# Gates and ups of a GEGLU FFN as pairs of 64-row half tiles, beside a sliding-window attention

## The chip, the cores and the metric

The kernel runs on one core of one Trainium2 chip. The metric is the device time of one execution in microseconds. TensorE (PE) multiplies matrices, VectorE (DVE), ScalarE (ACT) and GpSimd (POOL) work element by element, and SyncE (SP) issues DMAs. Each engine works through its own instructions in order. TensorE writes to PSUM, which has eight banks of 128 partitions by 512 float32.

## The reference

The input x is 2048 rows of D = 448, in bfloat16. It is normalised once, and both halves of the sum read the normalised rows.

```python
xn  = layernorm(x)                                 # no scale, no shift
q, k, v = split(xn @ wqkv)                         # H = 16 heads, Dh = 28
scores  = einsum("bhqd,bhkd->bhqk", q, k) * Dh ** -0.5
mask    = (i - j >= 0) & (i - j < 256)             # sliding window of 256 keys
o       = softmax(where(mask, scores, -1e9)) @ v
ffn     = (gelu_tanh(xn @ w_gate) * (xn @ w_up)) @ w_down    # F = 1792
out     = x + o @ wo + ffn
```

## The kernel before, in words

The work goes in four blocks of 512 query rows (`qb`), one behind the other. Activations lie transposed: `xnT` holds xn with its features on the partitions, in four chunks. 448 features are three chunks of 128 and a rest of 64; the rest's 64 rows are stored in both halves of the fourth chunk. Each block has two parts.

*Attention* (`attention`, lines 536 to 662). A loop over steps, 10 in blocks 1 to 3 and 12 in block 0. A step's scores (L616) go to one tile of four banks, ScalarE takes their exp (L622) to `p_sb`, and masks follow on VectorE (L523) or, in block 0, on GpSimd (L533). There is one such score tile, so the scores of a step wait for the exp of the step before. At fixed steps (`pvs`) the product with v of a group of four heads is issued (`pv`, L576). From block 1 on it has two accumulators, one for each half of the keys, which ScalarE copies (L560) and VectorE adds (L561). These two are issued at once, or put in the list `behind`, which `flush` empties behind the next exp or gated multiply: group 2 in every block, and group 3 in block 3 alone. What depends on the sums (L548 to L556, and L542 on GpSimd) comes some steps later. Between the steps TensorE gets other work from feeds (`Feed`, generators that yield an estimate in ns behind each piece): in block 0 the rest of its q and k projections, some early ups and the projections of block 1; in blocks 1 and 2 the output projection and down matmuls of the block before (`gen_down`, L375 and L380) and the next block's projections; in block 3 the down of block 2 and early ups. `share` deals out the pieces by the estimates, with a share for each step (`want`) and a plan for the second feed (`plan`). What is left behind the last scores is drained at once.

*The gated part* (`gated`, L418 to L486). F = 1792 is 14 tiles of 128 columns, taken in pairs of neighbours (f, f + 1). Gates go to a tile of two banks (`gt`), ups to two single banks (`u0`). ScalarE takes the gelu of both gates (L464), and VectorE multiplies with the ups (L471), or with early ups already in `hT` (L469), where `gen_up` has had them copied by VectorE (L415). Early are f = 2, 4, 8 in block 0 and f = 2, 4, 6, 8, 10 in block 3. `last_v` issues the last PV group within the gated part, behind the first gates and ups. Behind each pair, `hook` issues what is left of the attention and, up to block 2, what the next blocks need: DMAs that gather and spread parts of k (`collect`, `deliver`), and in the first two blocks normalised rows and their DMA transposes.

A gate or up tile has a contraction of 448: three matmuls of 128 rows by 512 columns (`mm3`, L232) and one of 64 rows (`mm_half`, L238). Two such halves in the upper and lower 64 rows of the array run at the same time, and the kernel puts halves of two tiles next to each other. In blocks 1 to 3 the first pair's halves are cut to 32 columns of weights (m = 32), the shape of the PV matmuls behind them. The half's weights of w_gate and w_up lie in two tiles, `wgu3` and `wug3`.

*PSUM.* Four banks for scores and gates ("s"), two "m", one "o", one "d". `bank` takes the next name from a list (`ring`): in block 0 ("m", "m", "d"), later "m" alone. In block 0 the PV always uses "o". After block 3 comes its own down (`gen_down`), a check of the softmax sums, and an alternative path for unusual inputs, which isn't run here.

The loads of x and weights are DMAs on SP's queue, a few small ones on ScalarE's, in the order of the code. Transposes of the first four row tiles are done by TensorE (`transp`), later ones by DMA.

Of the kernel before, what the change touches and what calls it, by code (L numbers as in the profile page):

```python
# [9 lines left out]
ALU = mybir.AluOpType  # L10
# [6 lines left out]
P = 128  # L17
# [58 lines left out]
def kernel(  # L76
# [45 lines left out]
    def rows(w, c0, n):  # L122
        return w[c0 * P:(c0 + n) * P, :].rearrange("(c p) n -> p c n", p=P)

# [19 lines left out]
    nc.sync.dma_start(out=wu[:, :, :], in_=rows(B_w_up, 0, 3))  # L144
    nc.sync.dma_start(out=wug3[0:64, :], in_=B_w_up[384:448, :])
    nc.sync.dma_start(out=wgu3[64:128, :], in_=B_w_up[384:448, :])
# [34 lines left out]
    xnT = const.tile([P, 4, S], bf16, name="xnT")  # L181
    qT = const.tile([P, 4, S], bf16, name="qT")
# [174 lines left out]
    UP1 = 1660  # L357
    STEP, PV = 450, 870
# [35 lines left out]
    def half(ps, f, gate, hi, ts, start, stop, m=P):  # L394

        w3 = wgu3 if gate != bool(hi) else wug3
        mm_half(ps, w3[:, f * P:(f + 1) * P], xnT[:, 3, ts], hi, start, stop, m)

    def three(ps, f, gate, ts, start, stop):
        w = wg if gate else wu  # L400
        mm3(ps, lambda c: w[:, c, f * P:(f + 1) * P], lambda c: xnT[:, c, ts], start, stop)

    def gen_up(qb, fs):

        ts = slice(qb * QB, (qb + 1) * QB)
        for f in fs:
            us = []
            for i in range(2):
                us.append(bank("ue"))
                three(us[i][:, :], f + i, False, ts, True, False)  # L410
                yield (650, HOLD) if i else 650
            for i in range(2):
                half(us[i][:, :], f + i, False, i, ts, False, True)
            for i in range(2):
                nc.vector.tensor_copy(out=hTs[qb][:, f + i, :], in_=us[i][:, :])  # L415
            yield -360

    def gated(qb, early, last_v, flush, hook):  # L418

        ts = slice(qb * QB, (qb + 1) * QB)  # L420
        hT = hTs[qb]
        turn = ["o" if down_tag[0] == "d" else "d", down_tag[0]] * 4

        def single(name, tag):
            return psum.tile([P, QB], f32, name=name, tag=tag, bufs=2 if tag == "m" else 1)[:, :]

        def begin(f, apart=False):
            last_tag[0] = turn[0] if f not in early else last_tag[0]
            pr = dict(f=f, us=[])
            if apart:  # L430
                pr["gs"] = [single("g0", tag) for tag in ("m", turn.pop(0))]
                return pr
            pr["gt"] = phase[0].pool.tile([P, 2, QB], f32, name="gt", tag="s")
            pr["gs"] = [pr["gt"][:, i, :] for i in range(2)]
            if f not in early:
                tags = ("m", turn.pop(0))
                if qb == 0 and f == 0:
                    tags = [ring[0][(ring[1] + i) % 3] for i in range(2)]
                    if "d" in tags:
                        turn.insert(0, "o")  # L440
                pr["us"] = [single("u0", tag) for tag in tags]
            return pr

        def dense(pr, start):
            f = pr["f"]
            gs = [(g, f + i, True) for i, g in enumerate(pr["gs"])]
            us = [(u, f + i, False) for i, u in enumerate(pr["us"])]
            for ps, fi, gate in (gs + us if f else us + gs):
                three(ps, fi, gate, ts, start, not start)

        def halves(pr, start, m):
            f = pr["f"]
            for i in range(2):
                if pr["us"]:
                    half(pr["gs"][i], f + i, True, 0, ts, start, not start, m)
                    half(pr["us"][i], f + i, False, 1, ts, start, not start, m)
                else:
                    half(pr["gs"][i], f + i, True, i, ts, start, not start, m)

        def end(pr):  # L460
            f = pr["f"]
            ge = work.tile([P, 2, QB], bf16, name="ge", bufs=2)
            if "gt" in pr:
                nc.scalar.activation(out=ge[:, :, :], in_=pr["gt"][:, :, :], func=ACT.Gelu_apprx_tanh)  # L464
            else:
                for i, g in enumerate(pr["gs"]):
                    nc.scalar.activation(out=ge[:, i, :], in_=g, func=ACT.Gelu_apprx_tanh)
            if not pr["us"]:
                nc.vector.tensor_tensor(out=hT[:, f:f + 2, :], in0=ge[:, :, :], in1=hT[:, f:f + 2, :], op=ALU.mult)  # L469
            for i, u in enumerate(pr["us"]):  # L470
                nc.vector.tensor_tensor(out=hT[:, f + i, :], in0=ge[:, i, :], in1=u, op=ALU.mult)  # L471
                flush()
            hook(f)

        for fs in ((0, 2), (4, 8, 6), (10, 12)) if qb in (0, 3) else ((0,), (2, 4), (6, 8), (10, 12)):
            prs = [begin(fs[0])]
            dense(prs[0], True)
            prs += [begin(f, len(fs) == 3 and f == fs[1]) for f in fs[1:]]
            for pr in prs:
                halves(pr, pr is not prs[0], 32 if qb and not fs[0] else P)  # L480
            if not fs[0]:
                last_v()
            end(prs[0])
            for pr in prs[1:]:
                dense(pr, False)
                end(pr)  # L486
# [49 lines left out]
    def attention(qb, feeds, aux, plan):  # L536
# [30 lines left out]
        def pv(g):  # L567

            tags = ("o",) if not qb else ("m", "m" if g < 3 else down_tag[0])
# [22 lines left out]
        pvs = {4: 0, 6: 1, 9: 2} if qb else {4: 0, 7: 1, 10: 2}  # L592
        for i, (scores, ncol, edges) in enumerate(steps):
# [111 lines left out]
    transp(3, nc.vector.tensor_copy, "d")  # L705
    pvs.append(alone("pv", "o"))
# [17 lines left out]
    ring[1] = 0  # L724
# [20 lines left out]
    def loads():  # L745

        nc.sync.dma_start(out=x_sb[:, 12:16, :], in_=xv[:, 12:16, :])
        nc.sync.dma_start(out=wgu3[0:64, :], in_=B_w_gate[384:448, :])
        nc.sync.dma_start(out=wug3[64:128, :], in_=B_w_gate[384:448, :])
        nc.sync.dma_start(out=wg[:, :, :], in_=rows(B_w_gate, 0, 3))  # L750
# [7 lines left out]
    for qb in range(NB):  # L758
# [80 lines left out]
    with tc.If(n_ok < 1, preferred_fallthrough_block=True, label="general"):  # L839
        general_path(tc, locals_=dict(x_sb=x_sb, xnT=xnT, qT=qT, kT=kT, v_sb=v_sb, wg=wg, wu=wu, wgu3=wgu3, wd=wd, wo=wo,  # L840
                                      ident=ident, outv=outv))


def general_path(tc, locals_):
# [4 lines left out]
    with ExitStack() as st:  # L849
# [11 lines left out]
        for qb in range(NB):  # L861
            ts = slice(qb * QB, (qb + 1) * QB)
            for f in range(NF):
                fs = slice(f * P, (f + 1) * P)
                pg = ps.tile([P, QB], f32, name="pg", tag="pg")
                pu = ps.tile([P, QB], f32, name="pu", tag="pu")
                for i, (dst, w) in enumerate(((pg, L["wg"]), (pu, L["wu"]))):
                    for c in range(3):
                        nc.tensor.matmul(dst[:, :], lhsT=w[:, c, fs], rhs=xnT[:, c, ts], start=(c == 0), stop=False)
                    p0 = 64 * i  # L870
                    nc.tensor.matmul(dst[:, :], lhsT=L["wgu3"][p0:p0 + 64, fs], rhs=xnT[p0:p0 + 64, 3, ts], start=False, stop=True,
                                     tile_position=(p0, 0))
# [78 lines left out]
```

## Time and profile before

| | |
|---|---|
| median of 3 runs | 220.65 us (220.32 to 220.88) |
| the profiled execution | 221.15 us, of which the span is 219.4 |
| mean granted TensorE clock | 0.996 |
| TensorE busy | 213.9 us, 2287 matmuls |
| VectorE, ScalarE, GpSimd busy | 152.1, 133.3, 46.9 us |
| exp (L622) | 42 times, 73.8 us in all |
| gelu (L464) | 26 times, 1.02 us each |
| copy of a PV accumulator (L560) | 12 times, 0.58 us each |
| copy of an early up (L415) | 16 times, 10.2 us in all |
| DMA | 13.30 MB, engines busy mostly in the first 45 us |

The span is what the trace shows from the first instruction to the last; the execution's own time has 1.7 us around it. "Issue" in the lists of waits is time in which an engine waited for nothing that the profile shows. A line that names a helper (L232, L238) stands for all that call it, so groups are told apart by their tiles: `gt` gates, `u` ups, `ue` early ups, `po` output and down, `sc` scores, `ov` PV. PEld is TensorE's loading of weights, which runs beside the matmuls.

### The profile page before, as it was taken

To read this page: it belongs to the slowest core of one execution; us is meant where nothing else is said; L and a number is where in the kernel's file an instruction comes from. 1 tells how busy PE (TensorE), PEld (TensorE's weight loads), DVE (VectorE), ACT (ScalarE), POOL (GpSimd) and SP (SyncE) were. 2 spreads that over 40 slices of the span, in tenths; PEclk is the share of its full clock that TensorE was granted. 3 is DMA by queue.
4 is the path that set the end of the run, shared out by engine and by line. 5 is a ranking of instruction groups with operands and counts; after the bars stand their busy time and mean duration, and the time that the engine had idled before them with its cause. 6 is when DMAs were issued, how large, how long until landed. Compare 5 with 4: busy or idle time off the path is not lost.

```text
span 219.4 us, 5447 instructions
## 1 busy us (share of the span) xinstructions
PE 213.9 (98%) x2287; PEld 96.1 (44%) x2287; DVE 152.1 (69%) x346; ACT 133.3 (61%) x131; POOL 46.9 (21%) x80
## 2 busy tenths in 40 slices
PE   7999999999999999999999999999999999999993
PEld 2433333434444454444444445444344445444562
DVE  6787896799666883679565795386356799479521
ACT  3588788662878875432878888233486777565000
POOL 5377987320000120022000022022000022022001
PEclk9999999999999999999999999999999999999998
DMA  6993799104200001102300000200000000000011
GB/s 193 310 311 71 188 325 302 30 4 72 45 3 21 24 24 27 20 3 46 60 13 24 23 1 24 52 13 0 0 3 21 25 3 24 24 1 0 22 35 37
DMA packets 18045, 13.30 MB, mean 61 GB/s; under 512 B 8704, under 2 KB 16992, under 8 KB 18016
## 3 DMA queue, kind: packets, MB, share of 16 engines
q1 hardware_dynamic: 17072, 12.62, 21.1%
q8 instruction: 19, 0.31, 0.6%
q10 hardware_dynamic: 944, 0.29, 0.5%
q14 instruction: 10, 0.08, 0.1%
HBM read 9.15 MB, written 2.18 MB: 52 GB/s over the span
## 4 chain that ended last, share of the span: by engine, by line
PE 96%; ACT 1%; DVE 1%; issue 1%; DVEq 0%
PE po L380 20%; PE gt L232 16%; PE u L232 12%; PE sc L616 6%; PE po L375 6%; PE gt L238 5%; PE ue L232 5%; PE ov L576 5%; PE pq L232 4%; PE pv L232 4%; PE pk L232 3%; PE wps L191 2%; PE pq L238 1%; PE g L232 1%; PE ue L238 1%; PE pv L238 1%
## 5 line engine op out<-in xcount | busy, mean ns | idle before, releaser
L622 ACT ACTIVATE p_sb<-sc 128x2048 bf16<-128x2048 f32 (+2 forms) x42 | 73.8, 1758 | 12.6 <-PE sc L616 8.2
L380 PE MATMUL po<-wd,hT 128*128 128x448 bf16 (+1 forms) x238 | 49.8, 342 | 0.0
L464 ACT ACTIVATE ge<-gt 128x1024 bf16<-128x1024 f32 x26 | 26.6, 1024 | 34.9 <-PE u L238 20.1
L542 POOL TENSOR_TENSOR oN<-oc,l 128x512 bf16<-128x512 f32 x12 | 16.0, 1334 | 137.8 <-DVE l L556 87.4
L232 PE MATMUL gt<-xnT,wg 128*128 128x512 bf16 x156 | 37.5, 380 | 0.0
L471 DVE TENSOR_TENSOR hT<-ge,u 128x512 bf16<-128x512 bf16 x40 | 25.7, 682 | 12.9 <-ACT ge L464 12.9
L380 PEld LDWEIGHTS <-hT 128*128 128x128 bf16 x238 | 21.5, 98 | 18.8 <-issue 2.6
L232 PE MATMUL u<-xnT,wu 128*128 128x512 bf16 x120 | 29.2, 379 | 0.0
L523 DVE TENSOR_TENSOR p_sb<-p_sb,masks 128x256 bf16<-128x256 bf16 (+1 forms) x90 | 26.8, 353 | 0.4 <-ACT p_sb L622 0.4
L232 PEld LDWEIGHTS <-wg 128*128 128x128 bf16 x168 | 15.3, 98 | 21.3 <-issue 4.5
L232 PEld LDWEIGHTS <-wu 128*128 128x128 bf16 x168 | 16.0, 98 | 19.2 <-issue 1.0
L561 DVE TENSOR_TENSOR oc<-oc,ov 128x512 f32<-128x512 f32 x12 | 8.2, 687 | 16.5 <-ACT oc L560 16.5
L616 PE MATMUL sc<-qT,kT 28*64 28x320 bf16 (+7 forms) x640 | 16.9, 263 | 0.2
L415 DVE CAST hT<-ue 128x512 bf16<-128x512 f32 x16 | 10.2, 681 | 8.4 <-PE ue L238 8.3
L375 PE MATMUL po<-wo,oN 128*128 128x448 bf16 (+1 forms) x68 | 15.9, 343 | 0.0
L385 DVE TENSOR_TENSOR res<-po,x_sb 128x448 bf16<-128x448 f32 (+1 forms) x17 | 10.0, 586 | 8.6 <-PE po L380 8.4
L533 POOL TENSOR_SCALAR_AFFINE_SELECT p_sb<-p_sb 128x512 bf16<-128x512 bf16 (+1 forms) x20 | 14.2, 730 | 5.0 <-ACT p_sb L622 4.8
L238 PE MATMUL gt<-xnT,wgu 64*128 64x512 bf16 (+1 forms) x67 | 12.7, 380 | 0.0
L560 ACT COPY oc<-ov 128x512 f32<-128x512 f32 x12 | 7.0, 583 | 8.8 <-PE ov L576 8.8
L232 PE MATMUL pq<-xnT,wqp 128*128 128x512 bf16 x45 | 12.2, 380 | 0.1
L548 DVE STREAM_TRANSPOSE l<-oc 128x512 f32<-128x512 f32 x16 | 11.3, 704 | 1.4 <-POOL oN L542 1.2
L232 PE MATMUL ue<-xnT,wu 128*128 128x512 bf16 x48 | 12.0, 380 | 0.0
(97 smaller groups left out, 241.9 us busy)
## 6 DMA issues: line engine op xcount, KB each, us to landing
out_dram<-res SPq DMA_DIRECT2D x15, 112.0 KB
x_sb<-in_A_x_dram SPq DMA_DIRECT2D x3, 448.0 KB
wu<-in_B_w_up_dram SPq DMA_DIRECT2D x1, 1344.0 KB
wg<-in_B_w_gate_dram SPq DMA_DIRECT2D x1, 1344.0 KB
wd<-in_B_w_down_dram SPq DMA_DIRECT2D x3, 448.0 KB
wraw<-in_A_wqkv_dram SPq DMA_DIRECT2D x2, 252.0 KB
wo<-in_A_wo_dram SPq DMA_DIRECT2D x4, 98.0 KB
wv<-in_A_wqkv_dram SPq DMA_DIRECT2D x1, 336.0 KB
```

Of the source, the lines that this page charges most:

```text
L232: nc.tensor.matmul(ps, lhsT=lhs(c), rhs=rhs(c), start=start and c == 0, stop=stop and c == 2, skip_group_check=True)
L238: nc.tensor.matmul(ps[c:c + m], lhsT=lhs[p0:p0 + 64, c:c + m], rhs=rhs[p0:p0 + 64], start=start, stop=stop, tile_position=(p0, c), skip_gr ...
L375: nc.tensor.matmul(po[:, 0:w], lhsT=oN[:, g, cs], rhs=wo[:, g, lo:up], start=(g == 0), stop=False, skip_group_check=True)
L380: nc.tensor.matmul(po[:, 0:w], lhsT=hT[:, f, cs], rhs=wd[:, f, lo:up], start=False, stop=(f == NF - 1), skip_group_check=True)
L464: nc.scalar.activation(out=ge[:, :, :], in_=pr["gt"][:, :, :], func=ACT.Gelu_apprx_tanh)
L471: nc.vector.tensor_tensor(out=hT[:, f + i, :], in0=ge[:, i, :], in1=u, op=ALU.mult)
L523: nc.vector.tensor_tensor(out=reg, in0=reg, in1=m, op=ALU.mult)
L533: nc.gpsimd.affine_select(out=reg, in_=reg, pattern=mid + [[1 if diag else -1, min(w, P)]], compare_op=ALU.is_ge, fill=0.0, base=0 if diag ...
L542: nc.gpsimd.tensor_tensor(out=oN[:, g, :], in0=oc[:, :], in1=inv, op=ALU.mult)
L548: nc.vector.transpose(out=l1[:, :, :].rearrange("p a b -> p (a b)"), in_=oc[:, :])
L616: nc.tensor.matmul(ss[k0:k0 + nk, j, col:col + nq], lhsT=kT[r, g, kt * P + k0:kt * P + k0 + nk], rhs=qT[r, g, qb * QB + q0:qb * QB + q0 + ...
L622: nc.scalar.activation(out=p_sb[:, :, 0:ncol], in_=ss[:, :, 0:ncol], func=ACT.Exp, scale=SCALE)
```

## The change

Gates and ups are no longer three matmuls of 128 rows and one of 64, but seven of 64 rows. F is cut in halves: tile p (0 to 6) pairs with tile p + 7. The weights of tile p lie in partitions 0 to 63 and those of p + 7 in partitions 64 to 127, each as seven chunks of 64 features. `chunk` issues the two matmuls of one chunk, one in each half of the array.

Each of the two needs the same 64 features of x, but in its own half of the partitions. Chunk c lies in only one half of `xnT`, so the other half comes from `xsw`, a copy of the block's x with the halves of the partitions exchanged, which two DMAs from SBUF to SBUF make (`swap`): in block 0 on ScalarE's queue, right behind the fourth transpose; in blocks 1 to 3 on SP's, ahead of the block's attention. There is one `xsw`, so each swap waits for the last reader of the one before.

Further:
- `load_ffn` loads w_up and w_gate by two DMAs each instead of three.
- Early are pairs 1, 2, 4 in block 0 and 1, 2, 3 in block 3. An early up takes both its banks at the start.
- The gated part's order is new: gates first, then ups, pair by pair, with pair 0 and pair 1 next to the last PV; the 32-column halves are gone.
- Block 0's ring has four banks behind its first six places, and its PV takes its bank from there. Its feed mixes early ups and v projections in another order.
- PV groups 2 and 3 go to `behind` in every block.
- Estimates, block 3's plan and the formula of the share in block 3 have other constants; the run of the first feed at the start of the attention is gone.

```diff
-    wg = const.tile([P, 3, F], bf16, name="wg")
-    wu = const.tile([P, 3, F], bf16, name="wu")
-    wgu3 = const.tile([P, F], bf16, name="wgu3")
-    wug3 = const.tile([P, F], bf16, name="wug3")
+    wg = const.tile([P, 7, F // 2], bf16, name="wg")
+    wu = const.tile([P, 7, F // 2], bf16, name="wu")
...
+    def load_ffn(dst, w):
+        wv64 = w.rearrange("(c p) n -> p c n", p=64)
+        for hi in range(2):
+            nc.sync.dma_start(out=dst[64 * hi:64 * hi + 64, :, :], in_=wv64[:, :, hi * (F // 2):(hi + 1) * (F // 2)])
...
-    UP1 = 1660
-    STEP, PV = 450, 870
+    UP1 = 1600
+    STEP, PV = 450, 700
...
+    def swap(qb, queue):
+        ts = slice(qb * QB, (qb + 1) * QB)
+        for hi in range(2):
+            queue.dma_start(out=xsw[64 * hi:64 * hi + 64, :, :], in_=xnT[64 - 64 * hi:P - 64 * hi, 0:3, ts])
+
+    def chunk(pair, w, p, qb, c):
+        for hi, ps in enumerate(pair):
+            r = slice(64 * hi, 64 * hi + 64)
+            ts = slice(qb * QB, (qb + 1) * QB)
+            x = xnT[r, 3, ts] if c == 6 else xnT[r, c // 2, ts] if c % 2 == hi else xsw[r, c // 2, :]
+            nc.tensor.matmul(ps, lhsT=w[r, c, p * P:(p + 1) * P], rhs=x, start=c == 0, stop=c == 6,
+                             tile_position=(64 * hi, 0), skip_group_check=True)
...
+        for p in ps:
+            us = [bank("ue")[:, :] for _ in range(2)]
+            for c in range(7):
+                chunk(us, wu, p, qb, c)
...
+                nc.vector.tensor_copy(out=hTs[qb][:, p + 7 * i, :], in_=us[i])
...
+        up(0)
+        gate(0)
+        end(0)
+        gate(1)
+        if 1 in early:
+            end(1)
+            gate(2)
+            up(2)
+        else:
+            gate(2)
+            up(1)
+            end(1)
+            up(2)
+        end(2)
+        for p in range(3, 7):
+            gate(p)
+            up(p)
+            end(p)
...
-            tags = ("o",) if not qb else ("m", "m" if g < 3 else down_tag[0])
+            if not qb:
+                ring[1] += 1
+            tags = (ring[0][ring[1] - 1],) if not qb else ("m", "m" if g < 3 else down_tag[0])
...
-                if g == 2 or qb == NB - 1 and g == 3:
+                if g > 1:
                     behind.append((oc, ov))
...
-        if qb:
-            feeds[0].run()
...
-                want = (whole - late) / (left + 0.2) + late - ahead - to
+                want = (whole - late) / (left + (0.2 if qb < NB - 1 else -0.4)) + late - ahead - to
...
-                share(feeds, want, to)
+                if qb == NB - 1:
+                    share(feeds[:1], want, 0)
+                    share(feeds, 0, to)
+                else:
+                    share(feeds, want, to)
...
     transp(3, nc.vector.tensor_copy, "d")
+    swap(0, nc.scalar)
...
-    ring[1] = 0
+    ring[:] = ["m", "m", "d"] * 2 + ["m", "o", "m", "d"] * 8, 0
...
-            early = (2, 4, 8)
+            early = (1, 2, 4)
...
-                          (gen_up(0, (2, 8)), 2 * UP1), (gen_proj(1), PROJ), (gen_up(0, (4,)), UP1))]
+                          (gen_up(0, (1,)), UP1), (gen_v(1, (4,)), 1500), (gen_up(0, (4,)), UP1), (gen_v(1, (6,)), 1500),
+                          (gen_up(0, (2,)), UP1), (gen_qk(1, range(4)), PROJ - 3000))]
...
-                early = (2, 4, 6, 8, 10)
+                early = (1, 2, 3)
...
-                plan = {0: 1300, 2: 1300, 4: 1300, 6: 1300, 7: 1300}
+                plan = {1: 1280, 2: 1280, 7: 1280}
+        if qb:
+            swap(qb, nc.sync)
```

More of the change, by code (lines that the diff above doesn't have):

```diff
@@ L143 @@
     nc.gpsimd.memset(v_sb[:, :, :, Dh + 1:32], 0.0)
[L144 to L146 removed]
+    load_ffn(wu, B_w_up)
     nc.sync.dma_start(out=x_sb[:, 8:12, :], in_=xv[:, 8:12, :])
@@ L181 @@
     xnT = const.tile([P, 4, S], bf16, name="xnT")
+    xsw = const.tile([P, 3, QB], bf16, name="xsw")
     qT = const.tile([P, 4, S], bf16, name="qT")
@@ L392, in new_hT @@
         hTs[qb] = hT
[L394 to L403, printed above, removed]
-        ts = slice(qb * QB, (qb + 1) * QB)
-        for f in fs:
-            us = []
-            for i in range(2):
[L409 to L416, printed above, removed]
+    def swap(qb, queue):
+        ts = slice(qb * QB, (qb + 1) * QB)
+        for hi in range(2):
+            queue.dma_start(out=xsw[64 * hi:64 * hi + 64, :, :], in_=xnT[64 - 64 * hi:P - 64 * hi, 0:3, ts])
@@ L421, in gated @@
         hT = hTs[qb]
         turn = ["o" if down_tag[0] == "d" else "d", down_tag[0]] * 4
[L424 to L464, printed above, removed]
-            else:
[L466 to L486, printed above, removed]
+        if not qb:
+            first = [ring[0][ring[1]], ring[0][ring[1] + 1]]
+            ring[1] += 2
+            turn = ["o" if "d" in first else "d", "d" if "d" in first else "o"] * 4
@@ new lines, in gated, with up, gate @@
+        us, ges = {}, {}
+        def up(p):
+            if p in early:
+                return
+            last_tag[0] = turn[0]
+            tags = ("m", turn.pop(0)) if qb or p else first
+            us[p] = [psum.tile([P, QB], f32, name="u0", tag=tag, bufs=2 if tag == "m" else 1)[:, :] for tag in tags]
+            for c in range(7):
+                chunk(us[p], wu, p, qb, c)
+        def gate(p):
+            gt = phase[0].pool.tile([P, 2, QB], f32, name="gt", tag="s")
+            for c in range(7):
+                chunk([gt[:, i, :] for i in range(2)], wg, p, qb, c)
+            if not p:
+                last_v()
+            ges[p] = work.tile([P, 2, QB], bf16, name="ge", bufs=2)
+            nc.scalar.activation(out=ges[p][:, :, :], in_=gt[:, :, :], func=ACT.Gelu_apprx_tanh)
@@ new lines, in end @@
+        def end(p):
+            ge = ges.pop(p)
+            if p in early:
+                nc.vector.tensor_tensor(out=both(hT, p), in0=ge[:, :, :], in1=both(hT, p), op=ALU.mult)
+            else:
+                for i, u in enumerate(us.pop(p)):
+                    nc.vector.tensor_tensor(out=hT[:, p + 7 * i, :], in0=ge[:, i, :], in1=u, op=ALU.mult)
+                    flush()
+            hook(2 * p)
+        up(0)
[11 more added lines that the diff above has]
+            up(2)
```

32 lines of the change are left out of this document (20 added, 12 removed).

## The prediction

> **What bounds the kernel now.** I read the page first: the busy shares, then the chain that ended last.
>
> ```profile
> span 219.4 us, 5447 instructions
> PE 213.9 (98%) x2287; PEld 96.1 (44%) x2287; DVE 152.1 (69%) x346; ACT 133.3 (61%) x131; POOL 46.9 (21%) x80
> PE 96%; ACT 1%; DVE 1%; issue 1%; DVEq 0%
> ```
>
> TensorE is busy 98% of the span and carries 96% of the chain. So a change pays only through fewer or shorter TensorE slots, and costs whatever it makes TensorE wait. Next the waits of TensorE's weight loads:
>
> ```profile
> PEld L238 <- issue: 16.8, 41, 0.4
> PEld L616 <- issue: 8.3, 32, 0.4
> PEld L232 <- issue: 6.8, 22, 0.4
> PEld L576 <- issue: 4.2, 12, 0.4
> ```
>
> Hardly any is a wait for another engine: they are "issue", and they come where the tile shape changes: L238 is the 64-row half, L616 the scores, L576 PV. What one costs is seen in TensorE's timeline in the gated part of block 0:
>
> ```profile
> 43.76 0.81 PE L232 MATMUL gt<-xnT,wg 128*128 128x512 bf16 x3
> 44.51 0.39 PE L238 MATMUL gt<-xnT,wgu 64*128 64x512 bf16 x1
> 44.51 0.39 PE L238 MATMUL gt<-xnT,wug 64*128 64x512 bf16 x1
> 44.73 0.38 PE L238 MATMUL g<-xnT,wgu 64*128 64x512 bf16 x1
> 44.74 0.38 PE L238 MATMUL g<-xnT,wug 64*128 64x512 bf16 x1
> 44.95 0.38 PE L238 MATMUL gt<-xnT,wgu 64*128 64x512 bf16 x1
> 44.95 0.38 PE L238 MATMUL u<-xnT,wgu 64*128 64x512 bf16 x1
> 45.16 0.38 PE L238 MATMUL gt<-xnT,wgu 64*128 64x512 bf16 x1
> 45.17 0.38 PE L238 MATMUL u<-xnT,wgu 64*128 64x512 bf16 x1
> 45.48 0.39 PE L232 MATMUL g<-xnT,wg 128*128 128x512 bf16 x1
> ```
>
> Columns: start, duration, instruction. Two 64-row matmuls start together and the next pair follows about 0.216 us later: a pair costs one slot, the same as a dense 128-row matmul of 512 columns (three in 0.81 with the last one's 0.38: 0.216 apart). From dense to pair it is 0.31 (the third dense starts at 44.19, the pair at 44.51), from pair to dense again 0.31 (45.17 to 45.48): a change of shape costs some 0.1.
>
> Last, the end of block 3's attention, all engines:
>
> ```profile
> 184.04 0.43 PE L616 MATMUL sc<-qT,kT 28*64 28x320 bf16 x24
> 184.40 2.82 PE L380 MATMUL po<-wd,hT 128*128 128x448 bf16 x14
> 184.64 1.88 ACT L622 ACTIVATE p_sb<-sc 128x2048 bf16<-128x2048 f32 x1 [0.83 <-PE sc L616]
> 186.41 0.58 ACT L560 COPY oc<-ov 128x512 f32<-128x512 f32 x1
> 187.02 0.69 DVE L561 TENSOR_TENSOR oc<-oc,ov 128x512 f32<-128x512 f32 x1 [0.56 <-ACT oc L560]
> 187.06 0.38 PE L232 MATMUL u<-xnT,wu 128*128 128x512 bf16 x1
> ```
>
> After the last scores, the first up needs the bank of PV group 2, which ScalarE empties (L560) only behind its last exp: 187.06 - 184.04 = 3.02 us. Fourteen output matmuls cover it just so; nothing is idle.
>
> **The slots.** Before, a pair of F tiles takes 2 x 6 dense slots and 2 paired ones, 14 in all; after, 2 x 7 paired ones, 14 again. Slot for slot the change gains nothing: 392 slots either way over the four blocks.
>
> **The switches (a gain).** From the order of the instructions, shape changes fall from 161 to 140. Mean extra gap of each kind, from the starts in the trace: dense to 64-row 99 ns (12 fewer: 1.19 us), back 99 (9 fewer: 0.89), dense to PV 96 (3 fewer: 0.29), 64x32 to dense 147 (3 fewer: 0.44), block-0 scores to dense 113 (3 fewer: 0.34), one each of block-0 PV to dense (113) and dense to scores (96): 0.21. Removed 3.36. Added are eleven, of kinds that mostly have no row; each is priced by the sibling with dense in the place of 64-row: 3 x 113, 3 x 147, 3 x 96, 1 x 113, 1 x 106 = 1.29 (bounds: all 96, 1.06; all 147, 1.62). Net -2.07; a first slot behind a switch is also 10 ns long, 21 x 10 = 0.21. Sum -2.28, bounds -1.9 to -2.6.
>
> **Weight loads.** Each slot now has two 64-row loads of 93 ns (group L238) in place of one of 98. I take 0: the shown pairs run on at 0.216 with such loads beside them. But those chains are four slots long, and the new ones 7 to 42. Bounds: 0, and for loads wholly exposed 336 slots that were dense x 93 ns = 31 us. I stay by the chain, which is the same operation.
> The Trainium skill, "TensorE: Matmul & The Clock Gate", Part 3, "What overlaps and what doesn't", says that a weight load overlaps running matmuls only when it targets another row group; here both row groups are busy, so by that rule the 31 us would show. This trace's 0.216 between pairs speaks against it.
>
> **The start and block 0 (a loss).** The ring of four banks makes the first projection of group 1 wait for VectorE's copy of the second v tile (12.58 + 0.61, from the timeline) where it had waited for ScalarE's of the first, and the one behind it moves along: 0.1 to 0.25, part of it within two waits that are there now (0.17 at 14.97, 0.12 at 15.37): +0.15. Between scores 4 and 5 the filler is 1.85 us against 0.39 + 1.45 + 0.05 that one exp and its hand-over take: +0.05 to 0.09. An early up's second matmul follows ScalarE's v copy: +0.08. Together +0.3 (0.1 to 0.5).
>
> **Copies by DMA (nothing).** Block 0's swap is two issues on ScalarE's queue, 0.40 to 0.55 us each by its earlier issues; they fall between VectorE's copy of the last transpose (9.47 + 0.42) and the statistics that ScalarE waits for until 11.41. Behind them stands only that rstd. Its 384 packets of 1 KB at 46 to 126 ns on 16 engines are 1.1 to 3.0 us more beside the up weights, which land by 16.33; the first early up is at 19.49. Cover left: 0.16 at least. Two DMAs of wu (1.8 KB packets) move the bytes of three before; 0.9 KB and 3.6 KB packets have nearly one rate (16 to 21 bytes/ns). Transposes 6 and 7, now behind the swap's semaphores on SP, are issued at 20.41 or later: 0. Blocks 1 and 2 read their swap 30 us later. Block 3's is issued when the last up of block 2 has run; the first early up comes 4.1 us behind that by the new order. Two issues of 0.5, then an output row's 1.68 from issue to landing plus 0.2 to 1.2 for the larger size: landed 2.4 to 3.4 us behind. Cover 0.7; I take 0, bounds 0 to 0.9. SP has only output stores queued behind it, the first of them later than this.
>
> **Block 3 (the main loss).** Early ups fall from five pairs to three: 2 x 7 slots of 0.216, 3.02 us, less filler under the attention's ten exps, which stay as they are (the two pairs' ups come later, in the gated part). Three places follow:
> - The second early pair starts close behind the first and, its halves running together, needs both banks "m" at once, so both VectorE copies (two L415, 1.29 us in a row) must be over; before, the next up began with one bank, and waited 0.10 (at 179.68). +0.58 (bounds 0.1 to 0.7).
> - Step 6 to 7 has 2.36 to 2.41 us of filler against 0.73 + 1.88 + 0.06 = 2.67 of hand-over and exp: +0.25 (0.18 to 0.35, with step 7).
> - The first up still waits for L560's copy, 3.02 after the last scores, but only six output matmuls are left as cover: scores 0.36 + 6 x 0.19 + 0.1 = 1.60. +1.35 (1.28 to 1.42). The filler was spent in earlier steps, the new share divides by left - 0.4 in place of left + 0.2.
> Together +2.18.
>
> **Blocks 1, 2 and the rest (nothing).** Cover behind their last scores is 3.54 against 3.02. The copies put behind a gelu delay group 3's sum by some 1 us; ScalarE idles 34.9 us ahead of its gelus, and the output projection that reads it comes a block later (in block 3, six gelus later). Without that cover it would cost one L560 and one L561, 1.27. VectorE's mults of early pairs are still one instruction each.
>
> **Sum.** -2.28 + 0.30 + 2.18 = +0.20. The profiled run took 221.15 (span 219.4 and 1.7 around it), 0.5 above the median of 220.65. So 221.35 in such a run, 220.85 as median.
>
> **Rivals.** A measurement of this kernel tells a change from none at about 0.3%, 0.66 us: 219.99 to 221.31 is "same".
> - *A, the forecast*: gain and waits cancel; 220.85, with its bounds 219.9 to 221.8.
> - *B, block 3 doesn't wait*: if ScalarE's copy isn't what the first up needs (another bank) and the copies of the early pairs keep up and the steps aren't short, the gain is left with the start's loss: -2.28 + 0.30 = 218.7; with half the waits 219.8. For it: the present block 3 has waits of 0.1 only. Against: 3.02 us hang on one exp and one copy, and the filler is counted.
> - *C, slower through the swapped copy in block 3*: TensorE takes its work in order, so each us that it lands past 4.1 us behind its release is a us on the end. Landing at 5.5 gives 222.2, at 7 223.7. For it: 1 KB packets here take 46 to 126 ns, over twice apart, and nothing shows an on-chip copy of this size. Against: the cover of 0.7. It decides from 4.6 us on.
> - *D, long chains of pairs run slower than 0.216*: 392 slots, so 4 ns more in each is 1.6 us, 222.4; 10 ns 3.9, 224.7; it decides from 1.2 ns on. Against: the four shown. Its far end, every load exposed, is 220.85 + 31 = 252; I give that 0.02 of D's 0.17.
> That far end is what the Trainium skill's page named above would have.
>
> **Chances.** A 0.46, B 0.24, C 0.13, D 0.17. A gives 0.02 faster, 0.36 same, 0.08 slower; B 0.23 faster and 0.01 same; C 0.13 and D 0.16 slower, 0.01 same. Faster 0.25, same 0.38, slower 0.37. Forecast 220.85. A's own range is 219.9 to 221.8; to hold 8 in 10 it must take in most of B and the near half of C and D: 218.7 to 222.6.
>
> **What will show it.** Shape changes: the L238-like issue waits fall, and pairs stand 0.216 apart in chains of any length (else D). The waits page should have a wait of TensorE's first up on ScalarE's oc copy of 1.3 us in block 3, and of an early up on VectorE's hT copy of 0.6 (else B); a wait on the swapped copy's DMA would be C. ScalarE's and VectorE's busy times should stay within 1 us. I'm wrong if block 3's attention doesn't lose about 2 us to waits, or the rest doesn't gain 2.

## The result, and the profile after

The changed kernel takes 223.39 us (median of 6 executions, 222.35 to 223.75) against 220.58 for the kernel before: 1.0116 times, 95% interval 1.0092 to 1.0141. It is slower, and above the range. The profiled execution took 223.43, span 221.6; that of before had 221.15 and 219.4. So the two profiled executions differ by 2.3 us, and their spans by 2.1, where the forecast had 0.2. (The profiled execution of before happened to lie 0.5 above its median, which is why the medians stand further apart.) In some kernels below single executions have a mean granted clock of 0.99 and take 1 to 4 us more; the ratios leave out those that are over 1.5% above the fastest of their kernel.

The page of the changed kernel:

```profile
span 221.6 us, 6054 instructions
PE 212.8 (96%) x2581; PEld 98.3 (44%) x2581; DVE 150.3 (68%) x344; ACT 132.9 (60%) x129; POOL 47.1 (21%) x80
PE 86%; DVE 5%; DMA 5%; ACT 2%; issue 2%; ACTq 0%; DVEq 0%
```

TensorE is busy 1.1 us less than before, and its share fell from 98% to 96%: what it saved, it waits, and more. In the chain stands a DMA with 5%, where there was none. The waits of TensorE's matmuls (who waited, for whom: us in total, times, longest) name the places:

```profile
PE wps L196 <- DVE wo L172: 1.4, 1, 1.4
PE u L413 <- ACT oc L563: 1.3, 1, 1.3
PE ue L413 <- DMA xsw<-xnT: 0.8, 1, 0.8
PE pq L237 <- DVE v_sb L263: 0.5, 2, 0.2
PE pv L237 <- DVE hT L431: 0.2, 1, 0.2
PE sc L619 <- ACT p_sb L625: 0.2, 1, 0.2
PE ue L413 <- DVE hT L431: 0.2, 1, 0.2
```

Only the first line was there before. The third is one that the prediction did not have. It stands in block 0 (timeline; start, duration, instruction):

```profile
19.55 0.40 PE L619 MATMUL sc<-qT,kT 28*128 28x128 bf16 x8
19.88 0.39 PE L413 MATMUL ue<-xnT,wu 64*128 64x512 bf16 x1
21.06 0.39 PE L413 MATMUL ue<-xsw,wu 64*128 64x512 bf16 x2 [0.79 <-DMA xsw<-xnT]
21.28 0.39 PE L413 MATMUL ue<-xnT,wu 64*128 64x512 bf16 x2
21.49 0.39 PE L413 MATMUL ue<-xsw,wu 64*128 64x512 bf16 x2
```

The first half of the pair needs only xnT and goes at 19.88. Its partner needs the swapped copy, and comes at 21.06. The two are 1.18 us apart: 0.96 of lost time, and one slot of 0.216 that runs alone, since the halves stay one step out of line until the end of the tile. The copy had been issued at 10.0 (ScalarE's timeline, then the piece of the chain):

```profile
10.02 1.54 ACTq L403 DMA_DIRECT2D xsw<-xnT  x2
11.61 0.30 ACT L206 ACTIVATE lnv<-mv_all,eps_t 128x2 f32<-128x2 f32 x1 [2.16 <-DVE mv_all L202]
```

```profile
10.73 10.20 DMA xsw<-xnT
```

10.2 us lie between the second issue and the landing at 20.93. The forecast had put the copy beside the weights at a cost of 1.1 to 3.0 us of their engines' time. In the packets of the trace, w_up's go from 9.35 to 18.88, and the copy's first one starts at 16.57, 5 us after it was issued; the last ends at 20.37. A packet of w_up, 1.8 KB, took 144 ns in the median, as long as one of 3.6 KB before the change (140).

The landing is not the end of the packets. In the traces a DMA raises its semaphore sixteen times, and TensorE goes on after the last: here fifteen of them stand by 20.64 and the last at 20.93, 0.56 behind the last packet.

The two issues took 1.54 us, not 0.8 to 1.1. At the start stands a wait on VectorE's copy of v. The first line is the changed kernel's; the second is from a kernel below (e7) in which ScalarE issues no DMA there:

```profile
13.29 0.81 PE L237 MATMUL pq<-xnT,wqp 128*128 128x512 bf16 x3 [0.22 <-DVE v_sb L263]
12.40 0.81 PE L237 MATMUL pq<-xnT,wqp 128*128 128x512 bf16 x3
```

In the first, VectorE's copy ends at 13.24; in the second it runs until 12.69, and the projection starts ahead of its end, right behind ScalarE's copy (12.35). So the projection waits for another engine in the two programs.

Block 3's end is as forecast:

```profile
183.36 0.43 PE L619 MATMUL sc<-qT,kT 28*64 28x320 bf16 x24
183.73 1.31 PE L385 MATMUL po<-wd,hT 128*128 128x448 bf16 x6
183.96 1.88 ACT L625 ACTIVATE p_sb<-sc 128x2048 bf16<-128x2048 f32 x1 [0.95 <-DVE l L559]
185.73 0.58 ACT L563 COPY oc<-ov 128x512 f32<-128x512 f32 x1
186.36 0.37 PE L413 MATMUL u<-xnT,wu 64*128 64x512 bf16 x1 [1.33 <-ACT oc L563]
```

From the last scores to the first up it is 3.00 us again, six output matmuls cover 1.6 of it, and TensorE stands for the rest.

Summed over the starts of the matmuls, waits and lone slots are 4.8 us after and 0.6 before, and the rest of the gaps fell by 2.2. Together that is +2.0 up to the last matmul, and 0.1 more behind it.

### The profile page after: what moved, and what is told of

The parts are those of the page before. It is cut to its first block, busy times and chain, and to the rows that moved or that the text cites. A ratio compares the mean times of both kernels' runs of the same rounds, so it can differ in the third digit from the quotient of the medians.

```text
span 221.6 us, 6054 instructions
## 1 busy us (share of the span) xinstructions
PE 212.8 (96%) x2581; PEld 98.3 (44%) x2581; DVE 150.3 (68%) x344; ACT 132.9 (60%) x129; POOL 47.1 (21%) x80
## 3 DMA queue, kind: packets, MB, share of 16 engines
HBM read 8.69 MB, written 2.18 MB: 49 GB/s over the span
## 4 chain that ended last, share of the span: by engine, by line
PE 86%; DVE 5%; DMA 5%; ACT 2%; issue 2%; ACTq 0%; DVEq 0%
PE gt L413 19%; PE po L385 18%; PE u L413 15%; PE po L380 6%; PE sc L619 5%; DMA xsw<-xnT 5%; PE ov L581 4%; PE pq L237 4%; PE ue L413 4%; PE pv L237 4%; PE pk L237 3%; PE wps L196 2%; DVE hT L431 1%; DVE p_sb L526 1%; PE pq L243 1%
## 5 line engine op out<-in xcount | busy, mean ns | idle before, releaser
L460 ACT ACTIVATE ge<-gt 128x1024 bf16<-128x1024 f32 x28 | 28.7, 1024 | 42.5 <-PE gt L413 41.5
L413 PE MATMUL gt<-xnT,wg 64*128 64x512 bf16 x224 | 45.6, 376 | 0.0
L468 DVE TENSOR_TENSOR hT<-ge,u 128x512 bf16<-128x512 bf16 x44 | 28.3, 679 | 21.0 <-PE u L413 12.6
L413 PE MATMUL gt<-xsw,wg 64*128 64x512 bf16 x168 | 40.7, 376 | 0.0
L413 PE MATMUL u<-xnT,wu 64*128 64x512 bf16 x176 | 36.6, 376 | 1.3 <-ACT oc L563 1.3
L413 PE MATMUL u<-xsw,wu 64*128 64x512 bf16 x132 | 32.0, 376 | 0.0
L413 PEld LDWEIGHTS <-wu 64*128 64x128 bf16 x392 | 19.3, 94 | 26.2 <-issue 5.9
L413 PEld LDWEIGHTS <-wg 64*128 64x128 bf16 x392 | 18.9, 94 | 22.6 <-issue 0.3
L619 PEld LDWEIGHTS <-kT 28*64 28x64 bf16 (+1 forms) x640 | 7.8, 102 | 11.5 <-issue 10.0
L263 DVE CAST v_sb<-pv 128x448 bf16<-128x448 f32 x13 | 7.7, 616 | 6.5 <-PE pv L243 6.5
```

The costliest lines, as they stand in the source:

```text
L413: nc.tensor.matmul(ps, lhsT=w[r, c, p * P:(p + 1) * P], rhs=x, start=c == 0, stop=c == 6, tile_position=(64 * hi, 0), skip_group_check=True)
L460: nc.scalar.activation(out=ges[p][:, :, :], in_=gt[:, :, :], func=ACT.Gelu_apprx_tanh)
L468: nc.vector.tensor_tensor(out=hT[:, p + 7 * i, :], in0=ge[:, i, :], in1=u, op=ALU.mult)
L619: nc.tensor.matmul(ss[k0:k0 + nk, j, col:col + nq], lhsT=kT[r, g, kt * P + k0:kt * P + k0 + nk], rhs=qT[r, g, qb * QB + q0:qb * QB + q0 + ...
```

## The experiments

**Block 0 without the copy (e1).**

```diff
-            x = ... if c % 2 == hi else xsw[r, c // 2, :]
+            x = ... if c % 2 == hi or not qb else xsw[r, c // 2, :]
...
-    swap(0, nc.scalar)
```

> Edit: block 0 has no swapped copy; its pairs read their own half of x where the swapped one belonged (so block 0's gates and ups are computed from wrong features; the matmuls are the same in number and shape). Theory T: the changed kernel lost 1.2 us in block 0 because the swapped copy landed at 21.0 us, behind the up weights' packets: the wait of 0.96 and the extra slot of 0.22 go, 223.4 becomes 222.2. Rival R: the next thing is late by then (the up weights, whose last packet ended at 18.9, or transposes 6 and 7), and takes the place of the wait: gain under 0.4, 223.0 or more.

222.56 us (1.0099 times before, 1.0077 to 1.0122). The profiled execution took 221.48, 1.95 less than that of the changed kernel; its trace has neither the wait on the copy nor those of the start: the gaps at 14.8, 15.2 and 18.9 us are 0.17, 0.12 and 0.14, those of the kernel before. Set side by side, matmul by matmul, the two traces are 0.2 apart at 6 us, ahead of the copy; another 0.4 come at the start, 1.2 at the copy's landing, and 0.2 behind the last matmul. So the copy costs 1.2 by its landing and some 0.4 by being issued on ScalarE's queue. In the medians it is less, 0.8 (0.4 by the ratios); the other three executions are 0.9 to 1.6 us longer than the profiled one, and what they wait for was not seen.

**The weights as DMAs of 128 partitions (e2).** Seven DMAs, one for each chunk, of 2 halves x 64 rows.

> Edit: w_up and w_gate are each loaded by seven DMAs of 128 partitions (one for each chunk of 64 features) in place of two of 64 partitions; packets stay 1.8 KB. If the 64 partitions are why a 1.8 KB packet took 144 ns (as much as one of 3.6 KB before the change): packets near 75 ns, the up weights in by 15 us, the swapped copy by 17, no wait: 222.2. If 1.8 KB rows out of 3.6 KB are slow by themselves, or the swapped copy's sharing of the engines: packets stay near 140 ns, the copy lands at 21 or later, and the time is 223.4 or up to 0.6 more for the five further issues on SP.

266.64 us (1.208). The experiment failed as one on time: TensorE waited eight times, some 4 us each, for chunks of weights, 32 us in all. But the packets say something: 74 ns for the same 1.8 KB, where few of them were under way at a time (some 25 start in a us, against 120). A 1.8 KB packet isn't slow by itself; whether the 128 partitions made it fast here or the small number, this run doesn't tell.

**Five early pairs in block 3 (e3).**

```diff
-                early = (1, 2, 3)
+                early = (1, 2, 3, 4, 5)
-                plan = {1: 1280, 2: 1280, 7: 1280}
+                plan = {1: 1280, 2: 1280, 4: 1280, 6: 1280, 7: 1280}
-                want = (whole - late) / (left + (0.2 if qb < NB - 1 else -0.4)) + late - ahead - to
+                want = (whole - late) / (left + (0.2 if qb < NB - 1 else 0.2)) + late - ahead - to
```

> Edit: block 3 has five early pairs (1 to 5) again instead of three, with plan steps 1, 2, 4, 6, 7 and the share's divisor left + 0.2. Theory T: block 3's waits (0.59 + 0.30 + 0.15 + 1.40) come from the 3.0 us of filler that it lost; with the filler back the first up has its cover again, and only the waits of an early pair for two banks stay, 0.2 to 0.2 each three times: 1.1 to 1.4 us less, 222.1. Rival: each early pair waits for both banks and both copies, 0.6 five times, and the gain is under 0.3: 223.1 or more.

222.56 us (1.0087, 1.0065 to 1.0109). Block 3 did what the theory said: of its waits 0.08 and 0.16 are left, at two early pairs, each with a lone slot. The total gained only 0.8 (0.6 by the ratios). In the profiled execution the wait on the copy was longer, 1.54 us (the time between the pair's starts less one slot), and something came behind it. The table by stretch (window; the last numbers are granted clock, DMA share, GB/s):

```profile
core 0: us, PE busy (x) PEld busy (x) DVE busy (x) ACT busy (x) POOL busy (x), PEclk, DMA share, GB/s
20.00:21.00 1.00, 0.06 (x2) 0.09 (x4) 0.00 (x0) 1.00 (x1) 0.64 (x2) 1.00 1.72 102
21.00:22.00 1.00, 1.00 (x7) 0.41 (x9) 0.00 (x0) 0.19 (x1) 0.74 (x1) 0.58 2.84 127
22.00:23.00 1.00, 1.00 (x8) 0.51 (x5) 0.00 (x0) 0.00 (x0) 1.00 (x3) 0.50 0.26 12
23.00:24.00 1.00, 1.00 (x13) 0.17 (x12) 0.45 (x1) 0.00 (x0) 1.00 (x8) 0.50 0.94 183
24.00:25.00 1.00, 1.00 (x20) 0.34 (x12) 0.94 (x3) 0.00 (x0) 0.34 (x3) 0.71 0.97 153
```

Right behind the idle stretch the clock was 0.50 for some 3 us, and pairs stood 0.42 apart in place of 0.216. Three us at half the rate are 1.5 us on top.

**Three early pairs, with the old divisor (e4).** The divisor of the last diff alone, left + 0.2.

> Edit: the changed kernel with the share's divisor in block 3 back at left + 0.2 (three early pairs, plan and feeds unchanged). Theory T: more output matmuls are left behind the last scores, the first up's wait of 1.40 goes and comes back as waits of 0.1 at four steps: 1.1 less, 222.3. Rival: the filler is 3 us short wherever it is put, so the waits move to the earlier exps and their sum stays: 223.4.

222.13 us (1.0067, 1.0047 to 1.0088), 1.26 less than the changed kernel (1.1 by the ratios). The theory had 1.1. TensorE's waits:

```profile
PE ue L413 <- DMA xsw<-xnT: 1.4, 1, 1.4
PE pq L237 <- DVE v_sb L263: 0.6, 2, 0.3
PE ue L413 <- DVE hT L431: 0.2, 1, 0.2
```

The line of the first up on ScalarE's copy is gone. A handful of score steps now start 0.1 to 0.2 late, and the second early pair's halves stand 0.6 apart as in the changed kernel. So the filler's lack costs less when it is spread: with divisor left - 0.4, output matmuls were spent under exps that were covered without them.

**Both waits gone (e5).** The edits of e1 and e4 together.

> Edit: block 0 without its swapped copy (its gates and ups use their own half of x and are wrong, same matmuls) and the share's divisor of block 3 at left + 0.2: the two long waits of TensorE, 1.0 to 1.5 us each, are both gone. Theory T: the two account for the loss and for the wide spread of the times (a wait of some 1.4 us let the granted clock fall to 0.5 for 3 us in one profile, which adds up to 1.5 us in such an execution): 223.4 - 1.5 - 1.1 = 220.8, and the executions lie within 0.7 us of each other as those of the kernel before do. Rival: the spread comes from somewhere else, stays above 1 us, and the median is 221.3 or more.

220.78 us over ten executions, 1.0017 times before (0.9997 to 1.0038). The median is as the theory said: the copy and the place of block 3's filler account for the loss, and what is left of the change neither gains nor loses here. The spread isn't: 220.06 to 222.14, where the theory had executions within 0.7; the profiled one, 220.64, has no wait over 0.4 apart from the 1.4 at the very start, which the kernel before has too. So the spread of e1 and e5 has another cause, which stays open.

**w_up on two queues (e6).** The second half on ScalarE's queue, the copy on SP's with x's rows 8 to 11 behind it, and the old divisor.

> Edit: the share's divisor at left + 0.2; the second half of w_up (64 partitions) is issued on ScalarE's queue, behind the copy of the first k weights; the swapped copy of block 0 and x's rows 8 to 11 follow on SP. Theory: a DMA into 64 partitions is limited to some 200 GB/s (1.8 KB packets at 146 ns on 16 engines, 74 ns where few ran), and two that write different halves run at the same time: packets under 110 ns, w_up in by 16, the copy by 18, no wait of the first early up: 221.0. Rival: the engines serve the second queue behind the first, or the limit is the source's: the copy lands at 20 to 21 as before, and the time is that of the share's divisor alone, 222.1.

221.88 us (1.007, 1.0045 to 1.0096); the rival's 222.1 is the nearer one. The packets: the first half's run from 9.1 to 13.9; the second half, issued by 9.2, starts at 12.7 and ends at 18.3. But for the last us of the first, the two queues did not run side by side. On either one a packet took 142 to 145 ns. In the profiled execution, the fastest with 221.18, the copy landed at 20.0 and its wait was 0.1; so where the other three, up to 222.72, lose their time was not seen.

**The copy as the last of SP's loads (e7).**

```diff
-    swap(0, nc.scalar)
+    swap(0, nc.sync)
```

> Edit: the changed kernel with block 0's swapped copy on SP's queue, behind all loads, in place of ScalarE's. Theory T (its packets run behind w_up's whichever queue they are on): the copy lands at 20 to 21.5 again, the wait of 1.0 to 1.5 stays, and only the two issues of 1.5 us that ScalarE made ahead of its statistics go, worth 0.3: 223.1. Rival: ScalarE's queue was served last, SP would have it in by 19: 222.0.

223.8 us (1.014, 1.0119 to 1.016). The start's gaps are those of the kernel before (0.17, 0.12, 0.14), so the start's loss hangs on ScalarE's issues. It isn't their time, though: in e4 ScalarE's statistics start at 11.46, right behind the VectorE result that they need, as before the change, and the projection waits 0.33 all the same. In every trace with a DMA issued there on ScalarE's queue (the changed kernel, e2, e3, e4, e6, e8, e9, e10) the projection's matmul waits for VectorE's semaphore, and in every one without (the kernel before, e1, e5, e7, e11, e12, e13, e14) for ScalarE's. So the issue changes which copy the built program waits for; how it comes to that is open.

The copy landed at 22.3. Its packets start at 18.17, behind w_up and most of x's rows 8 to 11, where on a queue of their own they had started at 16.57, beside x's rows and ahead of the k rest. The wait was 3.2, and the clock fell to 0.50 behind it. A queue of its own had thus been worth something.

**Two queues and five early pairs (e8).**

> Edit: as the one with w_up on two queues, and block 3 with five early pairs (plan steps 1, 2, 4, 6, 7). Theory: with five pairs the exps are covered again and only three waits of 0.2 for a bank stay, against four of 0.1 and one of 0.6 with three pairs: 0.1 to 0.2 less than with three, 220.9. Rival: more early copies load VectorE and its masks come later; 0.4 more than with three pairs, as the two single edits stood to each other, 221.4.

221.61 us over ten executions (1.0039, 1.0015 to 1.0064), 0.3 below e6: the theory's order, but the intervals overlap, so it isn't shown. Two of the ten had a clock of 0.99 and took 223.2 and 223.4, the profiled one among them, with a wait of 1.67 on the copy.

**Less of w_up at the start (e9, e10).** Only 640 of each half's 896 columns ahead, the rest behind w_gate.

```diff
-    load_ffn(wu, B_w_up)
+    load_ffn(wu, B_w_up, 0, 640)
...
         load_ffn(wg, B_w_gate)
+        load_ffn(wu, B_w_up, 640, F // 2)
```

> Edit: of w_up only the columns of tiles 0 to 4 of each half (640 of 896) are loaded at the start, the rest behind w_gate; the share's divisor of block 3 is left + 0.2. Everything is computed. Theory T: fewer bytes ahead of the swapped copy (1.15 MB for 1.6) bring w_up in by 16.5 and the copy by 18.5, before the first early up asks at 19.9: no wait on it, 221.0 (the start's 0.3 stays), and the executions lie within 1 us. Rival: 1.3 KB packets take as long as 1.8 KB ones, the copy lands at 20 or later and the time is that of the share alone, 222.1.

> Edit: the same split of w_up, with five early pairs in block 3 (plan steps 1, 2, 4, 6, 7, divisor left + 0.2). Everything is computed. Theory: no wait on the copy and only short ones in block 3, 220.8; that is the kernel before, 220.6, within 0.3%. Rival: w_up's load is still what block 0 waits for, 221.6 as with two queues.

With the old divisor (e9) seven executions lie at 220.3 to 221.7 (1.0015 times before, 0.9996 to 1.0034), and five at 223.8 to 224.9 with a clock of 0.99. With five early pairs (e10) nine lie at 219.9 to 220.7 (0.9993, 0.998 to 1.0006) and one at 224.1. w_up's last packet ends at 16.2 in both, but the copy still lands late: its packets end at 19.0 to 19.2, and the wait was 0.5 in e10's profile and 2.2 in e9's, which is one of the five. What differs is the last of the semaphore's sixteen steps. In e9 fifteen stand by 20.08 and the last at 21.67, 2.5 behind the last packet; in e10 it stands at 20.11. What held the last one up isn't shown. So the theory's time came in most executions, and its reason only in part.

**The kernel before, with w_up into 64 partitions (e11).**

```diff
-    nc.sync.dma_start(out=wu[:, :, :], in_=rows(B_w_up, 0, 3))
+    for h in range(2):
+        nc.sync.dma_start(out=wu[64 * h:64 * h + 64, :, :], in_=rows(B_w_up, 0, 3)[64 * h:64 * h + 64])
```

> Edit: in the kernel before, the three dense chunks of w_up come by two DMAs of 64 partitions each in place of one of 128; rows stay 3.6 KB, nothing else changes. If a DMA into 64 partitions is limited to about 200 to 250 GB/s: packets take 230 to 290 ns in place of 140, the last one ends at 18 in place of 15.5, and the time stays at 220.6 or rises by up to 0.6. If it is the row's length that made the 1.8 KB packets slow: packets stay at 140 ns.

221.17 us (1.0021, 1.0008 to 1.0035). The same 3.6 KB rows took 275 ns in place of 140, and the last one ended at 17.7 in place of 15.4. It is the 64 partitions. The Trainium skill says so: "SBUF — State Buffer", section "Door 1: The DMA port swizzle", has 64 partitions from 0 or 64 on at half the ports of all 128, and its section "Can I just issue two DMAs to hit both halves?" says that two DMAs, one for each half, serialise. This case's runs agree with both: 140 against 275 ns here, and e6's two queues one behind the other. The trace of the kernel before had a sign of it: w_up's dense packets took 140 ns in the median, and those of its last 64 rows, which go to 64 partitions in two tiles, 229, in the stretch from 13.0 us on. The forecast had read w_up's rate off rows by their size, not by their number of partitions.

**The kernel before, with three early pairs (e12).** f = 2, 4, 8 in block 3.

> Edit: the kernel before with early ups f = 2, 4, 8 in block 3 in place of 2, 4, 6, 8, 10; plan and shares unchanged. Theory: the waits of block 3 come from 3.0 us less filler under its exps, whatever the shape of the ups: the time rises by 2.5 to 3, 223.3. Rival: the kernel before spreads its filler so that fewer early ups cost little (its waits there are 0.1 in all): under 0.7 more, 221.2.

224.68 us (1.0175, 1.0136 to 1.0213). Two score steps wait for an exp, 1.6 and 1.2 us:

```profile
PE sc L616 <- ACT p_sb L622: 2.8, 2, 1.6
```

The clock stayed at 1.0 behind the first and was 0.50 behind the second, 2.5 us later. The rise is 4.0 us, 2.8 of it waits; the kernel of before, with its shape of ups, loses too when it has three early pairs. So block 3's loss comes from fewer early ups, not from their shape.

**The copy right behind w_up (e13, e14).** On SP's queue, with the k rest and x's rows 8 to 11 issued after it; in e13 with the shorter w_up and five early pairs, in e14 alone.

```diff
-    nc.sync.dma_start(out=x_sb[:, 8:12, :], in_=xv[:, 8:12, :])
...
-    for a in range(2):
-        nc.sync.dma_start(out=w3k[64 * a:64 * a + 64, :], in_=A_wqkv[384:448, D + 12 * Dh:2 * D])
...
-    swap(0, nc.scalar)
+    swap(0, nc.sync)
+    for a in range(2):
+        nc.sync.dma_start(out=w3k[64 * a:64 * a + 64, :], in_=A_wqkv[384:448, D + 12 * Dh:2 * D])
+    nc.sync.dma_start(out=x_sb[:, 8:12, :], in_=xv[:, 8:12, :])
```

> Edit: block 0's swapped copy on SP's queue right behind w_up and ahead of the k rest and x's rows 8 to 11 (not on ScalarE's); w_up's first 640 columns of each half at the start, the rest behind w_gate; five early pairs in block 3. Everything is computed. Theory T: without other loads between, the copy lands by 18, before the first early up (19.2 to 19.9): the wait of 0.5 to 2 and all executions with a clock of 0.992 go; ScalarE's two issues of 1.5 us go too, and with them 0.3 at the start: 219.5, 0.5% faster than the kernel before. Rival: the copy still lands at 19 or later, and the kernel stays where the split with five pairs was, 220.4, with single executions at 224.

> Edit: the changed kernel with this one edit: block 0's swapped copy on SP's queue right behind w_up, the k rest and x's rows 8 to 11 behind it. Theory T (order of the packets decides, and ScalarE's issues cost the start 0.3): against the copy as the last of SP's loads (223.8) and on ScalarE's queue (223.4), the copy lands at 19 to 20, wait 0 to 0.3: 221.9. Rival: w_up alone holds it back, it lands at 20.5 again with a wait of 0.8: 223.0.

Alone (e14) it is 222.89 us (1.0109, 1.0088 to 1.0129), as the rival said: the start has the gaps of the kernel before again, the copy's packets wait for nearly the whole of w_up (16.1, where w_up ends at 17.5), it lands at 19.9, and the wait is 0.96, since the first early up also comes 1.1 earlier. With the shorter w_up and five early pairs (e13) it is 219.95 us, 219.51 to 220.13, 0.9961 times before (0.9946 to 0.9976): faster than both kernels. Its page and all of its matmuls' waits:

```profile
span 218.3 us, 6056 instructions
PE 213.0 (98%) x2581; PEld 98.3 (45%) x2581; DVE 152.1 (70%) x346; ACT 132.8 (61%) x129; POOL 46.9 (21%) x80
```

```profile
PE wps L193 <- DVE wo L171: 1.4, 1, 1.4
```

The copy's packets run from 13.8 to 17.1 and it has landed before the first early up at 19.5. There is no wait on it, the mean granted clock is 0.998 or more in all six executions, and the spread is 0.6. Two early pairs of block 3 still start 0.08 and 0.16 late, as in e3. So the changed kernel gains once the copy is in time and block 3 has its filler back; by 0.9 us, not by all of the 2.2 that the switches save.

## Why the prediction was wrong

- *The slots, and the weight loads.* Right. Of the 378 steps from pair to pair inside a chain, 363 are 0.215 or 0.216 us, 13 are 10 ns longer, and two are waits. The chains are up to 84 slots long, where the forecast had counted 42. Rival D, with its exposed loads, fell.
- *The switches.* Right: 140 of them, the new kinds at 148, 113, 96, 109 and 106 ns, each like its sibling with dense. Forecast 2.28, left over in the traces 2.2.
- *The start and block 0*, +0.30. The step found the right place and the right wait, and the wrong reason. The first projection does wait for VectorE's v copy in place of ScalarE's, but the ring isn't why: with the same ring the wait is gone in e1, e7 and e14, where ScalarE issues no DMA. Start: 0.32 for 0.15. A v projection at 23.9 waits 0.32 for an early up's copy, a place that the forecast didn't have; that copy is itself late by the wait on the swapped copy.
- *Copies by DMA (nothing).* This is the step that failed: "Cover left: 0.16 at least." Instead of cover there was a loss of 1.18 us in the profiled execution (a wait of 0.96 and a lone slot), waits of 0.1 to 3.2 in the other profiles in which the copy came late, and half the clock behind the longer ones; e1, without the copy, and e13, with the copy in time, don't have it. Several sizes in the step were wrong. w_up in the new layout isn't as fast as before: with 64 partitions at a time a packet takes twice as long for its bytes, and the last one ends at 18.9, where the forecast had the load landed by 16.33. The copy wasn't carried beside w_up but almost behind it. Between its last packet and its landing lie another 0.6 us (up to 2.5 in e9), which the sum didn't have. And two issues on ScalarE took 1.54. The working took for granted that a second queue shares the engines evenly from its issue on. Only small transfers of ScalarE's queue stood beside SP's in the trace of before (4 to 6 us); no row had a second queue against a load like w_up's. With a cover of 0.16 the upper bound should have been some us, not zero.
- *Block 3*, +2.18. Right by place, and nearly by size: 0.59 for the second early pair (0.58), 0.30 and 0.15 for steps 6 and 7 (0.25), 1.40 for the first up (1.35), together 2.44. VectorE's busy time fell by 1.8 us, more than the 1 us that the signs allowed.
- *Rivals.* B fell: block 3 does wait. C named the right transfer in the wrong block: block 3's copy made nobody wait, as computed. The time went to 223.4 through block 0, a case that had no chance of its own, so the range ended below it. Of the 1.9 us that the span grew beyond the forecast, 1.2 are the copy's, and 0.3 each block 3's and the v projection's.

## What to carry to other kernels

A transfer whose cover is computed as a few tenths of a microsecond isn't free: look for rows in which two queues are full at the same time, and otherwise let the range hold the case that it comes behind all that was issued before it. A layout that loads into half of the partitions can be slower per byte (here 275 ns for 140); count the time until it has landed afresh, from rows with the same number of partitions, and order what the first consumer needs ahead of all that can come later. Filler that a tuned loop loses turns into waits; where they appear depends on its share, so a constant like left - 0.4 (1.1 to 1.3 us in e4) can be worth as much as the change itself.

## What was not expected of the hardware

- A wait of TensorE of about 1.5 us can cost as much again: behind waits of 1.54 (e3), 1.67 (e8), 2.2 (e9) and 3.2 (e7) the granted clock was 0.50 for some 3 us, and so it was in e12 behind 1.2 us that followed on 1.6; behind 0.96, 1.40 (in several profiles) and one of 1.54 (e4) it stayed at 1.0. The Trainium skill, "TensorE: Matmul & The Clock Gate", section "Why this matters for your kernels", advises to avoid gaps above about 3 us; here half of that was enough at times.
- Packets of a second queue started 5 us after their issue while the first queue was full (copy: issued by 11.6, first packet 16.57), and with w_up split over two queues the halves ran almost one behind the other (e6: the second, issued by 9.2, starts at 12.7).
- A DMA can land well behind its last packet: 0.56 us in the changed kernel, 1.5 in e4, 2.5 in e9, each time for the last of sixteen steps of its semaphore.
- Two copies of 192 KB from SBUF to SBUF took 0.67 and 0.83 us of ScalarE's time to issue, where its earlier DMAs had taken 0.40 to 0.55.
